# Decays of the first block from halves of 64 tokens: one running product of 512 columns per sequence, outer products and a masked spread on TensorE

## Chip, cores, metric

One core of one Trainium2 chip. The metric is the device time of one execution in microseconds, taken over several executions. All runs quoted here are of the state that the records call fast. Where two kernels are compared, the ratio is the mean time of one kernel's fast runs over that of the other's fast runs of the same rounds, so it is not quite the ratio of the medians beside it. "Faster" and "slower" mean below that the 95% interval of the ratio leaves out 1. The last three runs of the table of experiments ran on another chip, where the kernel before took 406.69 us; the eight before them on one chip.

## The reference

Two parts, one after the other. A Mamba-2 scan turns `x`, `a`, `B`, `C` (4 sequences, 8 heads, 768 tokens) into `y`, and a gated feed-forward block turns `y` into the output.

```python
# scan, per sequence and head: state decays by a[t], clipped to 1e-6..1
# y[i] = sum over j <= i of (C[i].B[j]) * (a[j+1]*...*a[i]) * x[j]   (plus the carried state)
h = x @ w_in            # 3072 x 256  @  256 x 2048
g = h * np.cos(h)
return (g @ w_out)      # 3072 x 2048 @ 2048 x 256
```

## The kernel before

Tokens go in six blocks of 128. The feed-forward block of block c runs while the scan of block c+1 is made, so only the scan of block 0 stands alone, ahead of everything else: this is the head that the change rewrites. For each sequence it needs the matrix `lam`, for 8 heads the 128 x 128 decays between every two tokens, got as running products along the columns. The decays `a` have to stand in all 128 partitions for that; TensorE spreads them with a column of ones. `fill` is a matmul without use, there to keep the array busy.

```python
def fill(dst, times=1):
    for _ in range(times):
        PE.matmul(dst, lhsT=ones, rhs=ones..., start=True, stop=True, ...)

def spread_a(b, tags):            # 4 heads to a bank of PSUM, two banks to a sequence
    ...
    for h in range(HH):
        r = (b_ * H + t * HH + h) * NC
        PE.matmul(a_ps[:, h], lhsT=ident[0:RB, r:r + 1].to_broadcast([RB, P]),   # RB = 96 rows
                  rhs=cut[:, u], start=(h == 0), stop=True, ...)

def decays(c, b, t):              # one scan of 512 columns: 4 heads x 128 tokens
    V.tensor_tensor_scan(out=lam[c, b][:, hs]..., data0=rows_..., data1=unit...,
                         initial=0.0, op0=ALU.mult, op1=ALU.add)
    ...

# turn: transposes B and C of a sequence (tp), ScalarE copies them (cT, bcT)
# intra: g = B.C on TensorE, then m = g * lam on VectorE (two instructions of 512 columns)
# finish: y = x.m on TensorE, copied to yT by ScalarE
# first: hp = w_in.yT, the first matmul of the feed-forward block
# grade, join: the weights, held as 64-bit floats, are made fp32 piece by piece

fill(bank([P, 4, P], "warm", "o"), 2)
spread_a(0, (None, "h"))
decays(0, 0, 0)
decays(0, 0, 1)
spread_a(1, ("o", "o"))
turn(0, 0)
decays(0, 1, 0)
decays(0, 1, 1)
intra(0, 0)
...                               # cut: the same for sequences 2 and 3
finish(0, 3, "o", 2)
...
for n in range(NC * NF + LAG):    # the body: first(n), gate(n), second(n - LAG), scan of block c+1
    ...
```

## Time and profile before

| | before |
|---|---|
| time, median of 6 runs | 407.28 us (407.03 to 407.63) |
| profiled span | 404.6 us |
| first hp matmul starts | 22.55 us |
| from there to the end | 382.1 us |

The prediction shows the main lines. Two more rows of the table by stretches matter later (columns: stretch, its length, busy us and count for PE, weight loads, VectorE, ScalarE, GpSimd, then granted clock, DMA share, GB/s):

```profile
6.00:12.00 6.00, 5.13 (x47) 4.52 (x46) 5.59 (x7) 0.78 (x3) 0.82 (x2) 1.00 1.00 108
12.00:18.00 6.00, 5.70 (x73) 4.04 (x72) 5.35 (x7) 3.36 (x10) 1.44 (x3) 1.00 1.05 340
```

### The profile page before, as it was taken

How to read it: one execution, taken by the hardware profiler on the slowest of the kernel's cores; microseconds unless marked ns; L12 is line 12 of the kernel's file. 1: busy time of each engine (PE TensorE's matmuls, PEld its weight loads, DVE VectorE, ACT ScalarE, POOL GpSimd, SP SyncE). 2: the span in 40 equal slices, each digit the busy share in tenths (PEclk: the TensorE clock that was granted, in tenths of full speed). 3: DMA queues.
4: the chain of work that ended last, by engine and by line, in shares of the span. 5: the costliest groups of instructions: out<-in, count | busy, mean ns of one | idle time of the engine just before them, and what ended most of it. 6: DMA issues, size and time to landing. Idle time of an engine off the chain costs nothing.

```text
span 404.6 us, 5703 instructions
## 1 busy us (share of the span) xinstructions
PE 397.9 (98%) x2166; PEld 254.3 (63%) x2166; DVE 257.7 (64%) x396; ACT 173.7 (43%) x329; POOL 48.1 (12%) x78
## 2 busy tenths in 40 slices
PE   8999999999999999999999999999999999999996
PEld 5646665666666666666656666666656565666664
DVE  6989999936666645676654666664566764433342
ACT  2576656534343434434334433433434343433332
POOL 2266655400000000000000000000000000000000
PEclk9999999999999999999999999999999999999999
DMA  7989999691111094110168211120100000100001
GB/s 112 301 229 221 221 272 146 169 104 53 52 54 52 17 143 75 53 52 2 52 107 77 75 31 53 52 78 3 52 2 0 0 2 0 53 0 0 2 0 53
DMA packets 106651, 30.55 MB, mean 75 GB/s; under 512 B 75328, under 2 KB 102528, under 8 KB 106624
## 3 DMA queue, kind: packets, MB, share of 16 engines
q1 hardware_dynamic: 106096, 29.92, 35.7%
q8 instruction: 17, 0.28, 0.3%
q10 hardware_dynamic: 528, 0.26, 0.2%
q14 instruction: 10, 0.08, 0.1%
HBM read 26.84 MB, written 3.34 MB: 75 GB/s over the span
## 4 chain that ended last, share of the span: by engine, by line
PE 97%; ACT 1%; DVE 1%; issue 0%; DVEq 0%
PE hp L378 42%; PE o L406 41%; PE g L309 4%; PE y L334 3%; PE y L325 2%; PE a_ps L258 2%; PE warm L94 1%; PE tp L291 1%; PE tp L290 1%; PE s_ps L351 0%; PE y L94 0%; ACT cT L295 0%; ACT w L389 0%; DVE m L313 0%; DVE gT L391 0%
## 5 line engine op out<-in xcount | busy, mean ns | idle before, releaser
L378 PE MATMUL hp<-yT,w_in 128*128 128x512 f32 x384 | 184.6, 604 | 0.7 <-DVE gT L391 0.7
L406 PEld LDWEIGHTS o<-w_out,gT 128*128 128x128 f32 x768 | 145.9, 190 | 59.9 <-issue 44.0
L406 PE MATMUL o<-w_out,gT 128*128 128x256 f32 x768 | 181.1, 379 | 0.0
L382 ACT ACTIVATE k<-hp 128x512 int32<-128x512 f32 x96 | 57.4, 598 | 125.9 <-PE hp L378 125.8
L384 DVE SCALAR_TENSOR_TENSOR w<-hp,k 128x512 f32<-128x512 f32 x96 | 66.0, 687 | 69.7 <-ACT k L382 68.4
L391 DVE TENSOR_TENSOR gT<-hp,w 128x512 f32<-128x512 f32 x96 | 66.3, 690 | 65.4 <-ACT w L389 65.4
L378 PEld LDWEIGHTS hp<-yT,w_in 128*128 128x128 f32 x384 | 67.9, 190 | 58.1 <-issue 53.8
L389 ACT ACTIVATE w<-w,quarter 128x512 f32<-128x512 f32 x96 | 69.3, 722 | 76.6 <-DVE w L384 76.6
L274 DVE TENSOR_TENSOR_SCAN lam<-arow,unit 128x512 f32<-128x512 f32 x40 | 49.0, 1226 | 0.0
L313 DVE TENSOR_TENSOR m<-g,lam 128x512 f32<-128x512 f32 x48 | 30.7, 681 | 0.9 <-PE g L309 0.7
L283 POOL TENSOR_TENSOR sc<-bc,lam 128x128 f32<-128x128 f32 x20 | 8.3, 413 | 122.5 <-DVE lam L274 79.5
L295 ACT ACTIVATE cT<-tp,slot 128x128 f32<-128x128 f32 x48 | 14.7, 356 | 9.4 <-PE tp L291 9.4
L309 PE MATMUL g<-cT,bcT 32*128 32x256 f32 x192 | 17.3, 426 | 1.2 <-ACT bcT L297 1.2
L334 PE MATMUL y<-m,xr 128*32 128x128 f32 x384 | 15.8, 279 | 0.2 <-DVE m L313 0.2
L369 POOL TENSOR_TENSOR state<-whole,slot 128x64 f32<-128x64 f32 x16 | 5.5, 343 | 79.3 <-DVE whole L366 79.3
L195 DVE SCALAR_TENSOR_TENSOR mag<-words,mag 128x512 uint32<-128x512 uint32 x16 | 13.2, 823 | 0.6
L175 POOL TENSOR_SCALAR mag<-mag 128x512 f32<-128x512 f32 x16 | 12.5, 783 | 7.5 <-ACT mag L174 7.5
L339 ACT COPY yT<-y 128x256 f32<-128x256 f32 x24 | 8.9, 371 | 10.2 <-PE y L334 10.1
L309 PEld LDWEIGHTS g<-cT,bcT 32*128 32x128 f32 x192 | 7.7, 182 | 8.8 <-issue 5.8
L334 PEld LDWEIGHTS y<-m,xr 128*32 128x32 f32 x384 | 8.8, 109 | 5.4 <-issue 3.6
L174 ACT ACTIVATE mag<-words 128x512 f32<-128x512 f32 x16 | 10.9, 683 | 1.7 <-DMA words<-in_moe_w_in_dram 1.7
L199 POOL TENSOR_TENSOR w_out<-mag,last 128x512 uint32<-128x512 uint32 x8 | 10.2, 1275 | 8.8 <-DVE mag L195 6.8
(49 smaller groups left out, 146.0 us busy)
## 6 DMA issues: line engine op xcount, KB each, us to landing
arow<-a_cut SPq DMA_DIRECT2D x20, 512.0 KB
words<-in_moe_w_in_dram SPq DMA_DIRECT2D x8, 512.0 KB
words<-in_moe_w_out_dram SPq DMA_DIRECT2D x8, 512.0 KB
out_dram<-ob SPq DMA_DIRECT2D x10, 256.0 KB
xr<-in_x_dram SPq DMA_DIRECT2D x4, 512.0 KB
along<-a_all SPq DMA_DIRECT2D x20, 64.0 KB
xr<-in_x_dram SPq DMA_DIRECT2D x8, 128.0 KB
bc<-in_B_dram SPq DMA_DIRECT2D x4, 256.0 KB
```

The source lines that it names most:

```text
L195: V.scalar_tensor_tensor(out=bits, in0=high, scalar=0xC0000000, in1=bits, op0=ALU.bitwise_and, op1=ALU.bitwise_or)
L274: V.tensor_tensor_scan(out=lam[c, b][:, hs].rearrange("p h i -> p (h i)"), data0=rows_.rearrange("p h i -> p (h i)"), data1=unit.rearrange ...
L295: ACT.activation(cT[:, t], tp[:, 1], AF.Copy, scale=slot[:, t:t + 1])
L309: PE.matmul(g[u // 2][:, u % 2, 0:2 * P], lhsT=bcT[r, 0], rhs=cT[r].rearrange("p t i -> p (t i)"), start=True, stop=True)
L313: V.tensor_tensor(out=m[:, hs].rearrange("p (k t) i -> p k (t i)", k=2), in0=g[u][:, :, 0:2 * P], in1=l[:, hs].rearrange("p (k t) i -> p k ...
L334: PE.matmul(y[32 * q:32 * q + 32, t], lhsT=xr[:, b, h], rhs=m[:, h], start=(c == 0 and t == 0), stop=True, tile_position=(0, 32 * q), skip ...
L378: PE.matmul(hp[n], lhsT=w_in[:, k, f * P:(f + 1) * P], rhs=yT[c][:, k], start=(k == 0), stop=(k == KT - 1))
L382: ACT.activation(k, hp[n], AF.Copy, bias=0.25, scale=INV_2PI)
L384: V.scalar_tensor_tensor(out=w, in0=hp[n], scalar=INV_2PI, in1=k, op0=ALU.mult, op1=ALU.subtract)
L389: ACT.activation(cos, cos, AF.Sin, bias=quarter, scale=TWO_PI)
L391: V.tensor_tensor(out=gT[n], in0=hp.pop(n), in1=cos, op=ALU.mult)
L406: PE.matmul(o[c][b], lhsT=g[:, b * P:(b + 1) * P], rhs=w_out[:, f], start=(f == 0 and (last or b % 2 == 0)), stop=(f == NF - 1), skip_grou ...
```

## The change

A block of 128 tokens is cut into two halves of 64. The two diagonal quarters of `lam` (both tokens in the same half) are made by one scan of 512 columns: the first half in partitions 0 to 63, the second in 64 to 127, 8 heads side by side. The quarter between the halves is an outer product: (decay from j to the end of the first half) times (decay from the start of the second half to i); TensorE makes it for 8 heads in one matmul, from operands in which masks leave each head only its own row. So VectorE needs four long scans instead of eight. The spread, too, is now a matmul over 32 masked rows (4 sequences x 8 heads). The core of the diff:

```diff
-    # cut: spread_a as it was, 56 passes of lhsT 96x128, rhs 96x128
+    def spread_a(b):
+        spread[b] = ps = bank([P, H, W], "a_ps", "h")
+        for t in range(2):
+            PE.matmul(ps[t * W:(t + 1) * W], lhsT=those[:, b], rhs=a0s[:, t], start=True,
+                      stop=True, tile_position=(0, t * W), skip_group_check=True)
+    def decays0(b):
+        lam[0, b] = l = scan.tile([P, 2, H, W], FP32, tag="lam", bufs=3, name="lam")
+        V.tensor_tensor_scan(out=l[:, 0]..., data0=spread.pop(b)..., data1=unit0..., ...)
+        G.tensor_copy(out=l[W:P, 1], in_=l[W:P, 0])
+        G.memset(l[W:P, 0], 0.0)
+    def cross(b):
+        ps = bank([W, H, W], "l_ps", "o")
+        PE.matmul(ps, lhsT=fros[:, b], rhs=tos, start=True, stop=True)
+        ACT.copy(out=lam[0, b][0:W, 1], in_=ps)
+        weigh(0, b)
 ...
+    # masks mine, those; short scans to, fro; masked operands a0s, fros, tos, all of 32 partitions
-    fill(bank([P, 4, P], "warm", "o"), 2)
+    fill(bank([P, 4, P], "warm", "o"), 3)
+    spread_a(1)
     turn(0, 0)
+    spread_a(2)
+    decays0(0)
+    decays0(1)
+    cross(0)
+    intra(0, 0, mult=False)
+    decays0(2)
+    cross(1)
+    spread_a(3)
+    gated(0, 0)
+    decays0(3)
+    turn(0, 1, "h")
+    cross(2)
+    finish(0, 0, "o", 1)
+    intra(0, 1)
 ...
+    cross(3)
+    turn(0, 2, "h")
     grade(*order[0])
 ...
+    join(*order[0])
     grade(*order[2])
-    join(*order[0])
```

The clip of the whole `a` and its stores move behind this, and the weights' first piece is fetched ahead of sequence 3's inputs.

More of the change, by code (lines that the diff above doesn't have):

```diff
@@ L63 @@
     LAG = 2
-    HP = H // 2
+    W = P // 2
+    NR = NB * H
     const = ctx.enter_context(tc.tile_pool(name="const", bufs=1))
@@ L132, in load_along @@
                 .to_broadcast([H, N, P]))
-    row0 = const.tile([P, HH, P], FP32, name="row0")
-    nc.scalar.dma_start(out=row0, in_=a[0, 0:HH, 0:P].unsqueeze(0).to_broadcast([P, HH, P]))
+    row0 = const.tile([P, H, W], FP32, name="row0")
+    a0 = const.tile([NR, P], FP32, name="a0")
+    nc.scalar.dma_start(out=a0, in_=a[:, :, 0:P].rearrange("b h p -> (b h) p"))
+    for t in range(2):
+        nc.sync.dma_start(out=row0[t * W:(t + 1) * W],
+                          in_=a[0, :, t * W:(t + 1) * W].unsqueeze(0).to_broadcast([W, H, W]))
     a_in = const.tile([RB, NU, P], FP32, name="a_in")
-    nc.sync.dma_start(
-        out=a_in, in_=a.rearrange("(u b) h (c p) -> (b h c) u p", u=NU, p=P))
     w_in = const.tile([P, KT, DF], FP32, name="w_in")
@@ L204 @@
         load(0, (b, b + 1))
-    for n in (0, 2, 1, 3, 4, 5):
+        if b == 1:
+            nc.sync.dma_start(
+                out=a_in, in_=a.rearrange("(u b) h (c p) -> (b h c) u p", u=NU, p=P))
+        if b == 2:
+            fetch(*order[0])
+    for n in (2, 1, 3, 4, 5):
         fetch(*order[n])
@@ L215 @@
     V.tensor_copy(out=unit, in_=ident.unsqueeze(1).to_broadcast([P, HH, P]))
+    unit0 = const.tile([P, H, W], FP32, name="unit0")
+    for t in range(2):
+        ts = slice(t * W, (t + 1) * W)
+        V.tensor_copy(out=unit0[ts], in_=ident[ts, ts].unsqueeze(1).to_broadcast([W, H, W]))
+    mine = const.tile([NR, H], FP32, name="mine")
+    G.tensor_tensor(out=mine, in0=ident[0:NR, 0:H], in1=ident[0:NR, H:2 * H], op=ALU.add)
+    for b in range(2, NB):
+        G.tensor_tensor(out=mine, in0=mine, in1=ident[0:NR, b * H:(b + 1) * H], op=ALU.add)
+    those = const.tile([NR, NB, W], FP32, name="those")
+    G.memset(those, 1.0)
+    G.affine_select(out=those, in_=those, pattern=[[-H, NB], [0, W]], compare_op=ALU.is_ge,
+                    fill=0.0, base=0, channel_multiplier=1)
+    G.affine_select(out=those, in_=those, pattern=[[H, NB], [0, W]], compare_op=ALU.is_ge,
+                    fill=0.0, base=H - 1, channel_multiplier=-1)
     own = const.tile([P, H], FP32, name="own")
-    V.memset(own, 1.0)
+    G.memset(own, 1.0)
     G.affine_select(out=own, in_=own, pattern=[[-N, H]], compare_op=ALU.is_ge,
@@ L224 @@
     slot4 = const.tile([P, HH], FP32, name="slot4")
-    V.tensor_tensor(out=slot4, in0=own[:, 0:HH], in1=own[:, HH:H], op=ALU.add)
+    G.tensor_tensor(out=slot4, in0=own[:, 0:HH], in1=own[:, HH:H], op=ALU.add)
     slot = const.tile([P, 2], FP32, name="slot")
-    V.tensor_tensor(out=slot, in0=slot4[:, 0:2], in1=slot4[:, 2:4], op=ALU.add)
-    cut = const.tile([RB, NU, P], FP32, name="cut")
-    G.tensor_scalar(out=cut, in0=a_in, scalar1=1.0, scalar2=1e-6, op0=ALU.min, op1=ALU.max)
-    G.memset(cut[:, :, 0:1], 0.0)
@@ L233 @@
-    la = const.tile([RB, NU, P], FP32, name="la")
-    V.tensor_scalar(out=la, in0=a_in, scalar1=1.0, scalar2=1e-6, op0=ALU.min, op1=ALU.max)
-    for dst, src in ((a_cut, cut), (a_all, la)):
-        nc.sync.dma_start(out=dst.rearrange("(u b) h (c p) -> (b h c) u p", u=NU, p=P), in_=src)
-    V.tensor_scalar(out=row0, in0=row0, scalar1=1.0, scalar2=1e-6, op0=ALU.min, op1=ALU.max)
+    G.tensor_tensor(out=slot, in0=slot4[:, 0:2], in1=slot4[:, 2:4], op=ALU.add)
+    ACT.activation(const.tile([P, 1], FP32, name="sine"), quarter, AF.Sin)
@@ new lines @@
+    clip = dict(scalar1=1.0, scalar2=1e-6, op0=ALU.min, op1=ALU.max)
+    V.tensor_scalar(out=a0, in0=a0, **clip)
+    to = const.tile([NR, W], FP32, name="to")
+    V.tensor_tensor_scan(out=to, data0=a0[:, W:P], data1=ones[0:NR, 0:W], initial=1.0,
+                         op0=ALU.mult, op1=ALU.mult)
+    fro = const.tile([NR, W], FP32, name="fro")
+    V.memset(fro, 1.0)
+    V.tensor_tensor_scan(out=fro[:, W - 2::-1], data0=a0[:, W - 1:0:-1],
+                         data1=ones[0:NR, 0:W - 1], initial=1.0, op0=ALU.mult, op1=ALU.mult)
@@ new lines @@
+    a0s = const.tile([NR, 2, H, W], FP32, name="a0s")
+    V.tensor_tensor(
+        out=a0s,
+        in0=a0.rearrange("p (t i) -> p t i", t=2).unsqueeze(2).to_broadcast([NR, 2, H, W]),
+        in1=mine.unsqueeze(1).unsqueeze(3).to_broadcast([NR, 2, H, W]), op=ALU.mult)
+    V.memset(a0s[:, :, :, 0:1], 0.0)
+    fros = const.tile([NR, NB, W], FP32, name="fros")
+    V.tensor_tensor(out=fros, in0=fro.unsqueeze(1).to_broadcast([NR, NB, W]), in1=those,
+                    op=ALU.mult)
+    tos = const.tile([NR, H, W], FP32, name="tos")
@@ L238 @@
+    for h in range(H):
+        ACT.activation(tos[:, h], to, AF.Copy, scale=mine[:, h:h + 1])
+    V.tensor_scalar(out=row0, in0=row0, **clip)
     V.memset(row0[:, :, 0:1], 0.0)
-    ACT.activation(const.tile([P, 1], FP32, name="sine"), quarter, AF.Sin)
     scaled, lam, reach, state, part, yT = {}, {}, {}, {}, {}, {}
@@ L246, in heads, with weigh @@
         return slice(b * H, (b + 1) * H)
-    spread = {}
-    def spread_a(b, tags):
-        u, b_ = b // (NB // NU), b % (NB // NU)
-        spread[b] = [] if b else [row0]
-        for t in range(len(spread[b]), 2):
-            a_ps = bank([P, HH, P], "a_ps", tags[t])
-            for h in range(HH):
-                r = (b_ * H + t * HH + h) * NC
-                PE.matmul(a_ps[:, h], lhsT=ident[0:RB, r:r + 1].to_broadcast([RB, P]),
-                          rhs=cut[:, u], start=(h == 0), stop=True, skip_group_check=True)
-            spread[b].append(a_ps)
+    spread = {0: row0}
+    def spread_a(b):
+        spread[b] = ps = bank([P, H, W], "a_ps", "h")
+        for t in range(2):
+            PE.matmul(ps[t * W:(t + 1) * W], lhsT=those[:, b], rhs=a0s[:, t], start=True,
+                      stop=True, tile_position=(0, t * W), skip_group_check=True)
+    def decays0(b):
+        lam[0, b] = l = scan.tile([P, 2, H, W], FP32, tag="lam", bufs=3, name="lam")
+        flat = "p h i -> p (h i)"
+        V.tensor_tensor_scan(out=l[:, 0].rearrange(flat), data0=spread.pop(b).rearrange(flat),
+                             data1=unit0.rearrange(flat), initial=0.0,
+                             op0=ALU.mult, op1=ALU.add)
+        G.tensor_copy(out=l[W:P, 1], in_=l[W:P, 0])
[5 more added lines that the diff above has]
+        weigh(0, b)
+    def weigh(c, b):
+        scaled[c, b] = sc = scan.tile([P, H, N], FP32, tag="sc", bufs=NB, name="sc")
+        l = lam[c, b][:, :, P - 1:P] if c > 0 else lam[c, b][:, 1, :, W - 1:W]
+        G.tensor_tensor(out=sc, in0=raw[c][0][:, 0, heads(b)],
+                        in1=l.to_broadcast([P, H, N]), op=ALU.mult)
     def reaches(c, b):
@@ L272, in decays @@
         hs = slice(t * HH, (t + 1) * HH)
-        rows_ = spread[b][t] if c == 0 else arow[c, b][:, hs]
+        rows_ = arow[c, b][:, hs]
         V.tensor_tensor_scan(
@@ L280, in decays @@
             return
-        scaled[c, b] = sc = scan.tile([P, H, N], FP32, tag="sc", bufs=NB, name="sc")
-        G.tensor_tensor(out=sc, in0=raw[c][0][:, 0, heads(b)],
-                        in1=lam[c, b][:, :, P - 1:P].to_broadcast([P, H, N]), op=ALU.mult)
+        weigh(c, b)
     def turn(c, b, tag=None):
@@ L300, in turn, with intra @@
         part[c, b] = (bcT, cT)
-    def intra(c, b):
+    def intra(c, b, mult=True):
         bcT, cT = part[c, b]
-        m = scan.tile([P, H, P], FP32, tag="m", name="m")
-        l = lam.pop((c, b))
         g = [pair("g") for _ in range(2)]
@@ L308, in intra, with gated, of @@
             r = slice(32 * u, 32 * u + 32)
-            PE.matmul(g[u // 2][:, u % 2, 0:2 * P], lhsT=bcT[r, 0],
-                      rhs=cT[r].rearrange("p t i -> p (t i)"), start=True, stop=True)
+            rhs = (cT[r].rearrange("p t i -> p (t i)") if c > 0 else
+                   cT[r].rearrange("p t (s i) -> p s t i", s=2))
+            PE.matmul(g[u // 2][:, u % 2, 0:2 * P], lhsT=bcT[r, 0], rhs=rhs,
+                      start=True, stop=True)
+        part[c, b] = (bcT, g)
+        if mult:
+            gated(c, b)
+    def gated(c, b):
+        bcT, g = part[c, b]
+        l = lam.pop((c, b))
+        m = scan.tile([P, H, P] if c > 0 else [P, 2, H, W], FP32, tag="m", name="m")
+        def of(t, u):
+            hs = slice(u * HH, (u + 1) * HH)
+            return (t[:, hs].rearrange("p (k t) i -> p k (t i)", k=2) if c > 0 else
+                    t[:, :, hs].rearrange("p s (k t) i -> p k s (t i)", k=2))
         for u in range(2):
-            hs = slice(u * HH, (u + 1) * HH)
-            V.tensor_tensor(out=m[:, hs].rearrange("p (k t) i -> p k (t i)", k=2),
-                            in0=g[u][:, :, 0:2 * P],
-                            in1=l[:, hs].rearrange("p (k t) i -> p k (t i)", k=2), op=ALU.mult)
+            in0 = g[u][:, :, 0:2 * P]
+            if c == 0:
+                in0 = in0.rearrange("p k (s i) -> p k s i", s=2)
+            V.tensor_tensor(out=of(m, u), in0=in0, in1=of(l, u), op=ALU.mult)
         part[c, b] = (bcT, m)
@@ L333, in finish @@
             q, t = h % 4, h // 4
-            PE.matmul(y[32 * q:32 * q + 32, t], lhsT=xr[:, b, h], rhs=m[:, h],
+            PE.matmul(y[32 * q:32 * q + 32, t], lhsT=xr[:, b, h], rhs=m[:, h] if c > 0 else m[:, :, h],
                       start=(c == 0 and t == 0), stop=True, tile_position=(0, 32 * q),
@@ L418, in second @@
             nc.sync.dma_start(out=rows_[:, 2 * i:2 * i + 2, c, :], in_=ob)
-    fill(bank([P, 4, P], "warm", "o"), 2)
-    spread_a(0, (None, "h"))
-    decays(0, 0, 0)
-    decays(0, 0, 1)
-    spread_a(1, ("o", "o"))
-    turn(0, 0)
-    decays(0, 1, 0)
-    decays(0, 1, 1)
-    intra(0, 0)
-    spread_a(2, ("h", "h"))
-    decays(0, 2, 0)
-    decays(0, 2, 1)
-    turn(0, 1)
-    finish(0, 0, "o")
-    intra(0, 1)
+    fill(bank([P, 4, P], "warm", "o"), 3)
+    spread_a(1)
+    turn(0, 0)
+    spread_a(2)
[5 more added lines that the diff above has]
+    cross(1)
+    cut = const.tile([RB, NU, P], FP32, name="cut")
+    la = const.tile([RB, NU, P], FP32, name="la")
+    spread_a(3)
[4 more added lines that the diff above has]
+    finish(0, 0, "o", 1)
+    intra(0, 1)
+    V.tensor_scalar(out=la, in0=a_in, **clip)
+    G.tensor_scalar(out=cut, in0=a_in, **clip)
+    G.memset(cut[:, :, 0:1], 0.0)
+    for dst, src in ((a_cut, cut), (a_all, la)):
+        nc.sync.dma_start(out=dst.rearrange("(u b) h (c p) -> (b h c) u p", u=NU, p=P), in_=src)
+    cross(3)
+    turn(0, 2, "h")
     grade(*order[0])
-    spread_a(3, ("o", "h"))
-    decays(0, 3, 0)
-    decays(0, 3, 1)
-    turn(0, 2, "h")
     finish(0, 1, "o", 1)
```

## The prediction

> **What bounds the kernel now.** I read the activity rows of the page first, then the table of busy time by stretches, then the chain that ended last, in order of time, for the first 32 us, then the timeline of each engine there, and the groups with shapes kept apart for durations.
>
> ```profile
> PE   8999999999999999999999999999999999999996
> DVE  6989999936666645676654666664566764433342
> ```
>
> TensorE (PE) is busy in nearly every slice of 10 us. Busy is not bound, so the stretches come next (columns: stretch, length, then busy us and count for PE, weight loads, VectorE, ScalarE, GpSimd, then clock, DMA share, GB/s):
>
> ```profile
> 18.00:24.00 6.00, 5.83 (x53) 2.79 (x53) 5.80 (x10) 3.75 (x9) 3.74 (x4) 1.00 0.90 257
> 24.00:30.00 6.00, 5.31 (x46) 2.67 (x45) 4.76 (x9) 5.07 (x9) 3.49 (x5) 1.00 0.81 242
> 30.00:36.00 6.00, 6.00 (x24) 3.94 (x23) 5.97 (x12) 3.25 (x6) 4.60 (x4) 1.00 0.98 195
> 60.00:80.00 20.00, 20.00 (x111) 12.45 (x110) 19.10 (x32) 11.99 (x24) 9.78 (x12) 1.00 0.93 154
> ```
>
> From 30 us on PE has no idle time. Three rounds of the second stage repeat every 12.7 us there (hp starts at 39.1 and 51.8), and their PE work is 3 x (1.91 + 1.73) plus about 1.8 of block work, 12.7. So the body is PE's own work and this change does not touch it. What can move is the start of the body, the first hp matmul at 22.55. That head is a chain through four sequences:
>
> ```profile
> 4.91 3.29 PE a_ps L258 x24
> ...
> 10.00 1.98 PE a_ps L258 x16
> ...
> 13.78 1.98 PE a_ps L258 x16
> ...
> 17.00 0.72 PE g L309 x8
> ...
> 18.35 0.69 DVE m L313
> 19.05 0.04 issue
> 19.09 0.43 PE y L334 x8
> 19.52 0.64 PE g L309 x8
> 20.16 1.06 PE y L94 x4
> 21.22 0.74 PE y L334 x16
> 21.96 0.63 PE warm L94 x2
> 22.59 1.92 PE hp L378 x4
> ```
>
> Here the reader is to see that the head, too, is mostly PE in its program order: spreads of the decays (a_ps), transposes, g, y. VectorE enters at 17.75 to 19.05 (m of sequence 2) and, hidden behind the filler matmuls at 20.16, at 20.19 to 21.48 (m of sequence 3). It is nearly full as well, with 5.80 of 6 us. Thus two engines are close to the bound in the head, and relief on one pays only until the other holds.
>
> [...]
>
> ```profile
> L265 DVE TENSOR_TENSOR_SCAN reach<-along,ones 128x128 f32<-128x128 f32 x20 | 10.3, 516 | 0.0
> L274 DVE TENSOR_TENSOR_SCAN lam<-a_ps,unit 128x512 f32<-128x512 f32 x7 | 8.1, 1206 | 0.3 <-PE a_ps L258 0.3
> ```
>
> 384 more columns cost 690 ns, 1.8 ns per column. [...] the trace has 681 (m) and 690 (gT). [...] sixteen y passes of 128 columns in four groups take 0.64 us with their latency, although one such pass takes 0.124 us in a_ps (1.98/16). [...] four filler passes of 512 columns from 1.12 on take 3.78 us, the same width later 1.91; the clock row, full throughout, does not show it.
>
> **Removed.** Of eight scans of 512 columns for block 0, four go: 4 x 1.2 = 4.8 us of VectorE. The 56 spread passes go from PE: 3.29 + 1.98 + 1.98 = 7.25 us. The masks (slot and own) move from VectorE to GpSimd, 0.4 us.
>
> **Added on VectorE before the first scan.** Two copies for unit0, 0.43 each as the present copy (L215); the clip of a0, about 0.2; two scans of 64 columns, about 0.3 to 0.4 each by the slope above; [...] small memsets, 0.2. Row a0 should land near 2.9, as a_in does now (wait ends at 3.09). [...] the clip of row0 (0.43, L237) and its memset 6.1. So the first scan starts at about 6.1 against 4.94 now: 1.2 of the 4.8 us are given back at once, and VectorE nets about 3.5 us less.
>
> **Added on PE.** Three spreads, each two fp32 matmuls of 512 columns. One fp32 matmul is two passes of 0.43 (hp: 1.91/4, start to start 0.43), so 0.87; the two column tiles go side by side, about 1.0 with weight loads. Four outer products (cross), 0.87 to 0.9 each. Sum 3 x 1.0 + 4 x 0.9 = 6.6 us against 7.25: **PE gains almost nothing.** One more filler of 512 columns stands at the start and one of 256 columns (two passes, 0.46 with their loads) before y of sequence 0.
>
> **Added elsewhere.** ScalarE: four copies of 64x512 from PSUM (about 0.5 each, from ob's 0.565) and eight small ones (0.25 each, before 6 us, harmless). GpSimd: per sequence one copy of 64x512 (0.6 to 0.9 from L175) and one memset (0.5), behind the scans, with room. DMA: row0 keeps its 256 KB but in pieces of half the size; the weights' first piece goes ahead of sequence 3's inputs. DMA is full from 2 to 22 us before and after; the last weights and the stores of a_cut keep their time, and the decays of block 1, first read at 33.5, have some microseconds to spare.
>
> **The new path in time**, all starts estimated from the durations above. The six passes of the filler: four start 0.85 apart from 1.12, the next at 4.7 and 5.55, ending near 6.2 as the clock comes up. Then in PE's program order: spread 1 to 7.2, transpose 0 (0.22) 7.4, spread 2 8.4, cross 0 9.3, g0 (0.64 to the next start now) 9.9, cross 1 10.8, spread 3 11.8, transpose 1 12.0, cross 2 12.9, filler 13.4, y0 (0.4) 13.8, g1 14.4, cross 3 15.3, transpose 2. Nothing waits long there: scans 0 to 2 run at 6.1 to 10.0, m0 till 11.3, scan 3 from 11.9 to 13.1, and VectorE then **idles** for g1 until about 14.5. ScalarE copies cross 3 (till 15.9), then cT and bcT of sequence 2 (0.8 from start to end, 8.45 to 9.23 now): g2 starts at 16.75, now 17.00. From there the old structure holds: m2 is over 1.8 later, y2 and the release of g's banks give g3 at 2.35 to 2.45 after g2 (17.00 to 19.45 now), 19.1; the first joining of weights stands before m3 as now (1.2 us); hp follows g3 by 3.1 (19.45 to 22.55): **22.2**. With spreads and crosses at 0.87 each it is 21.7. So the PE reading saves 0.35 to 0.85 us, not 3.5.
>
> **Rivals.** (a) VectorE is what bounds the head; then its net relief of 3.5 us arrives whole and hp starts near 19.0, total 403.9. For it: the two gaps in the chain at VectorE and its 5.8 of 6 us. Against it: the 9 us of PE work counted above lie in order between 6.2 and 15.3. I give it 0.15, a halfway outcome (PE gets ahead of its estimate, -1.5 to -2.5) 0.2. (b) ScalarE's order becomes the bound: cross copies stand before cT and bcT, and 2 x 1.2 us of weight conversion (pitch 0.59 each activation) lie between sequence 2's and the end; hp near 22.5, no change. For it: the conversion of the first piece, which was done at 15 us, now follows transpose 2. 0.25. (c) The side-by-side tiles do not hold[...]: three times 0.86 more, hp near 24, total 409. Against it: y's passes. 0.08. (d) The earlier body runs into transfers not yet landed: the saving is hidden; with only 0.5 us to lose it makes 407.4 at worst.
>
> **Range and chances.** The body moves one for one with hp. 0.5 x (-0.6) + 0.15 x (-3.5) + 0.2 x (-1.5 to -2) + the rest near 0 or +1 gives about -1.0: 407.4 - 0.9 = **406.5 us**, 8 in 10 between 404.7 and 407.9. 2% is 8.1 us, more than a third of the head, so within 2% has 0.97, faster 0.02, slower 0.01.
>
> **What would show it.** Right: four scans from about 6 us at 1.2 each; the spread in four passes within 1.1 us; a0s 1.2 us; PE without long gaps from 6 to 15 us; VectorE idle ahead of m1 and m2, waiting for g; first hp between 21.5 and 22.3; the body's length from the first hp to the end, 382.1 now, the same within 0.3. Wrong: hp before 20.5 (rival a), or cT of sequence 2 waiting behind other ScalarE work (b), spreads of 1.8 us (c), or a DMA wait at 25 to 35 us and a longer body (d).

The sum for the first scan came to 5.2 us for the end of a0s, 5.6 for that of fros and, with the clip and the memset, 6.1. The trace before gives about the same two costs as an estimate: operations of two inputs on VectorE take 0.292 us at 128 columns (bcT) and 0.681 at 512 (m; gT 0.690), which is 1.01 ns per column, so 1.20 us for the 1024 columns of a0s and 0.42 for the 256 of fros.

## The result and the profile after

The changed kernel takes 413.49 us (median of 6 runs, 411.61 to 414.74), the kernel before 407.28. The ratio is 1.0148, 95% interval 1.0112 to 1.0183. It is slower by 6 us, and its runs spread over 3 us, those of before over 0.6. They fall in two groups: 411.6 to 412.3, with a mean granted clock of 0.983 to 0.988, and 414.7 with 0.978 to 0.979. The profiled one is of the second group.

The activity rows of its page:

```profile
PE   8999999999999999999999999999999999999996
DVE  7258999964766763767673576764566665444442
PEclk9569999999999999999999999999999999999999
```

TensorE's row is as full as before. The row below is what is new: in the second and third slices the granted clock is at 5 to 6 tenths. By stretches, same columns as above:

```profile
6.00:12.00 6.00, 6.00 (x25) 1.78 (x25) 4.71 (x6) 1.36 (x4) 4.48 (x9) 0.87 0.98 138
12.00:18.00 6.00, 6.00 (x10) 1.30 (x7) 1.54 (x2) 1.94 (x5) 2.32 (x5) 0.50 0.97 226
18.00:24.00 6.00, 6.00 (x39) 2.62 (x42) 1.49 (x3) 2.11 (x6) 1.03 (x4) 0.50 0.99 351
24.00:30.00 6.00, 6.00 (x64) 3.17 (x53) 3.56 (x6) 4.45 (x11) 2.14 (x3) 0.71 0.68 142
```

TensorE counts as busy all the time, and its clock is halved from 10.5 to 27.5 us. VectorE, the engine that was to be relieved, works 1.5 of 6 us and waits for TensorE. The trace's clock record has these moments: full from 7.06, half from 10.47, full again from 27.54 us. The stretch at half clock is 17.07 us. The chain that ended last shows each piece at both speeds (columns: start us, us, what):

```profile
8.22 1.00 PE a_ps L297 x4
9.23 0.85 PE l_ps L314 x2
...
12.74 1.71 PE a_ps L297 x3
...
15.06 1.89 PE l_ps L314 x2
...
20.29 1.90 PE l_ps L314 x2
...
23.66 1.01 PE y L407 x16
24.67 1.24 PE g L369 x8
```

An outer product (l_ps) takes 0.85 us at 9.23 and 1.9 at 15.06 and 20.29; y takes 1.01, in the kernel before 0.57 to 0.74. The first hp, in the timeline:

```profile
31.10 1.10 PE L451 MATMUL hp<-yT,w_in 128*128 128x512 f32 x2
```

It starts at 31.10, before at 22.55, 8.55 later. The body from there to the end takes 413.0 - 31.10 = 381.9 us, before 382.1. So the whole loss of this execution lies in the head.

### The profile page after: what moved, and what is told of

Its sections match the earlier page's. It is cut to its first block, busy times and chain, and to the rows that moved or that the text cites. A ratio compares the mean times of both kernels' runs of the same rounds, so it can differ in the third digit from the quotient of the medians.

```text
span 413.0 us, 5679 instructions
## 1 busy us (share of the span) xinstructions
PE 407.8 (99%) x2134; PEld 252.0 (61%) x2134; DVE 256.2 (62%) x398; ACT 177.9 (43%) x341; POOL 56.8 (14%) x95
## 4 chain that ended last, share of the span: by engine, by line
PE 96%; DVE 2%; POOL 0%; issue 0%; ACT 0%; DVEq 0%; POOLq 0%
PE hp L451 41%; PE o L479 40%; PE g L369 4%; PE y L407 3%; PE y L398 2%; PE l_ps L314 2%; PE warm L95 1%; PE a_ps L297 1%; PE tp L350 1%; PE tp L351 1%; DVE mag L199 1%; PE y L95 0%; PE s_ps L424 0%; DVE mag L197 0%; POOL w_in L203 0%
## 5 line engine op out<-in xcount | busy, mean ns | idle before, releaser
L369 PE MATMUL g<-cT,bcT 32*128 32x256 f32 x192 | 18.5, 452 | 0.0
L407 PE MATMUL y<-m,xr 128*32 128x128 f32 x384 | 16.7, 293 | 0.0
L203 POOL TENSOR_TENSOR w_in<-mag,last 128x512 uint32<-128x512 uint32 x8 | 10.3, 1287 | 11.5 <-DVE mag L199 11.5
```

Of the source, the lines that this page charges most:

```text
L203: G.tensor_tensor(out=dst.bitcast(U32), in0=bits.rearrange("p (k f) -> p k f", k=k), in1=last.rearrange("p (k f) -> p k f", k=k), op=ALU.add)
L369: PE.matmul(g[u // 2][:, u % 2, 0:2 * P], lhsT=bcT[r, 0], rhs=rhs, start=True, stop=True)
L407: PE.matmul(y[32 * q:32 * q + 32, t], lhsT=xr[:, b, h], rhs=m[:, h] if c > 0 else m[:, :, h], start=(c == 0 and t == 0), stop=True, tile_p ...
```

## The experiments

The stretches of the clock record are 3.41, 17.07 and 385.7 us long in this trace, 1, 5 and 113 times 3.413 us, and 399.4 us in the kernel before, 117 times; such a step is called a window below. **Theory A**: the clock is halved because the new matmuls use few rows and columns of the array. TensorE is busy, but with 32 rows of 128 and, in the outer products, 64 columns of 128. **Theory B**: the array waits between instructions and so counts as idle, or what counts is the data, which are mostly zeros under the masks. Against the first half of B speaks already that the kernel before waited more (5.13 of 6 us busy) and kept its clock.

For theory A I estimated the use of the array in the changed kernel's one window at full clock, 7.06 to 10.47, from the durations of its chain: spreads 1.4 us (0.86 for the second by the passes' pitch of 0.43, the rest of the first) on a quarter of the array (32 rows, and 128 columns by two tiles side by side), transposes 0.22 us in full, an outer product 0.86 us on an eighth, g 0.3 us in full (four tiles of 32 rows): (0.35 + 0.22 + 0.11 + 0.3)/3.41 = 0.29, rounded to 0.3. In the same way I had 0.56 for the kernel before; a recount below gives 0.50 for its emptiest window.

All times, in the order in which they ran (first hp and span from the profiled execution):

| kernel | median us | ratio to before, interval | first hp | span less first hp |
|---|---|---|---|---|
| before (first 6 runs) | 407.28 | | 22.55 | 382.1 |
| changed | 413.49 | 1.0148 (1.0112 to 1.0183) | 31.10 | 381.9 |
| rows128 | 407.22 | 1.0001 (0.9986 to 1.0016) | 23.45 | 382.1 |
| before_rows32 | 413.89 | 1.0169 (1.0134 to 1.0204) | 31.41 | 382.6 |
| fillers | 410.73 | 1.0092 (1.0073 to 1.0112) | 26.99 | 382.1 |
| spread128 | 407.99 | 1.0017 (1.0002 to 1.0031) | 24.02 | 382.1 |
| cross128 | 407.68 | 1.0012 (0.9997 to 1.0028) | 24.12 | 382.1 |
| nofill | 406.56 | 0.9984 (0.9969 to 0.9998) | 23.06 | 382.1 |
| reordered | 405.75 | 0.9965 (0.9953 to 0.9978) | 21.82 | 381.8 |
| reordered2 | 405.57 | 0.9971 (0.9953 to 0.9989) | 23.55 | 381.8 |
| rows64 | 406.96 | 1.0010 (0.9993 to 1.0027) | 22.76 | 382.1 |
| cols128 | 412.11 | 1.0129 (1.0114 to 1.0144) | 28.26 | 381.8 |
| after_again | 414.72 | 1.0177 (1.0141 to 1.0213) | 30.83 | 382.2 |

The last column is the point of the table: in thirteen profiles the body takes 381.8 to 382.6 us. Whatever a kernel gains or loses, it does so ahead of the first hp.

### rows128: zeros in 96 more rows

```diff
-    a0 = const.tile([NR, P], FP32, name="a0")
+    a0 = const.tile([P, P], FP32, name="a0")
+    V.memset(a0[NR:2 * NR], 1.0)
+    V.memset(a0[2 * NR:P], 1.0)
     # mine, those, to, fro, a0s, fros, tos likewise [P, ...]; the masks make the added rows zero
```

> The changed kernel with the operands of its spreads and outer products padded from 32 to 128 partitions by rows of zeros; same passes, same result. Theory A, the array's clock is halved because what runs from 7 to 10.5 us uses few rows and columns of the array: the granted clock is 1.00 from about 7 us to the end, the first hp starts near 22.2 instead of 31.1, total 406.3 to 407.5. Theory B, the clock falls because TensorE waits between instructions, or because most of the data are zeros: nothing changes, 411.6 to 414.7.

The result is correct. The granted clock is 1.00 from 6.02 us to the end, and the 6 us are gone: 407.22 against 407.23 in the same rounds. The added rows hold zeros only, so neither the passes nor the useful data changed, and theory B falls in both its halves. From its chain:

```profile
7.76 1.01 PE a_ps L299 x4
8.77 0.85 PE l_ps L316 x2
...
12.50 1.00 PE l_ps L316 x2
...
15.35 1.00 PE l_ps L316 x2
```

The outer products stay at 0.85 to 1.00 us. The first hp starts at 23.45, where 22.2 was expected. And this is the fair test of the change's own idea: **with the clock kept, it gains nothing.** Its timeline shows why:

```profile
15.45 1.29 DVE L390 TENSOR_TENSOR m<-g,lam 128x512 f32<-128x512 f32 x2 [1.99 <-PE g L371]
...
18.58 1.29 DVE L390 TENSOR_TENSOR m<-g,lam 128x512 f32<-128x512 f32 x2 [1.64 <-PE g L371]
...
23.45 3.67 PE L453 MATMUL hp<-yT,w_in 128*128 128x512 f32 x8
...
28.77 1.52 PE L453 MATMUL hp<-yT,w_in 128*128 128x512 f32 x3 [1.07 <-DVE gT L466]
```

VectorE, with four scans less, idles 1.99 and 1.64 us for g (the bracket gives the idle time ahead of an instruction and what ended it). TensorE's program order holds the head.

### before_rows32: the same loss in the kernel before

```diff
-                PE.matmul(a_ps[:, h], lhsT=ident[0:RB, r:r + 1].to_broadcast([RB, P]),
-                          rhs=cut[:, u], start=(h == 0), stop=True, skip_group_check=True)
+                r = r % 32
+                PE.matmul(a_ps[:, h], lhsT=ident[0:32, r:r + 1].to_broadcast([32, P]),
+                          rhs=cut[0:32, u], start=(h == 0), stop=True, skip_group_check=True)
```

> The kernel before with its spread contracting over 32 rows instead of 96 (wrong decays on purpose, same passes and columns). Theory A: the clock falls to 0.50 about 9.5 us after the start for some windows, the first hp comes 4 to 9 us later, total 411 to 416. Theory B: 407.3 as the kernel before.

The result is wrong: heads get other heads' decays. The time is 413.89 us, as theory A expects, with nothing of the change in the kernel but the 32 rows. From its chain:

```profile
4.91 5.42 PE a_ps L259 x24
...
13.05 3.39 PE a_ps L259 x16
```

The kernel before has 3.29 and 1.98 there. One thing differs from what I wrote: in the profiled execution the clock did not rise and fall, it did not rise at all before 27.84 us. Its clock record begins with this rise, and the profile shows 1.00 for the 27 us ahead of it and a mean clock of 0.999. The durations show the half clock; the clock figure does not. It is the same in the kernel before, whose record begins at 6.05 us: the stretch from 0 to 6 us shows 1.00, and four passes of the filler took 3.78 us there, four of hp, as wide, 1.92 later. Two of the four runs (414.93 and 415.68 us) have this mean clock of 0.999; the other two (412.63 and 412.86) have 0.979, as of a clock that rose and fell. None of these two was profiled.

### fillers: more work, more speed

```diff
+    def busy(ps):
+        fill(ps.rearrange("p (k h) i -> p k (h i)", k=4)[:, 0:2], 1)
         spread[b] = ps = bank([P, H, W], "a_ps", "h")
+        busy(ps)
 ...                                  # and the same ahead of each outer product
```

> The changed kernel with one filler matmul of 128 rows, 128 columns and 256 moving columns ahead of each of the three spreads and four outer products: 7 x 0.43 = 3.0 us more work on TensorE. Theory A: the clock stays at 1.00, and hp starts near 24 to 25, total 408.5 to 410. If the fall has a cause outside the array's activity, the fillers only add: 414 to 418.

The clock is full from 4.94 us on, and the kernel is 2.8 us **faster** than the changed one although TensorE does seven matmuls more. At 410.73 us it is 0.7 above what I expected. The fillers took 0.43 us three times and 0.63 four times in its chain, 3.8 us and not 3.0; 26.99 - 3.8 = 23.2 is close to where rows128 has its hp, 23.45.

### spread128, cross128, rows64, cols128: how much is enough

```diff
# spread128: rows128, but cross with lhsT=fros[0:NR, b], rhs=tos[0:NR]
# cross128:  rows128, but spread_a with lhsT=those[0:NR, b], rhs=a0s[0:NR, t]
# rows64:    rows128, but [0:W] (64 rows) in both
# cols128:   the changed kernel, 32 rows, but
-    fros = const.tile([NR, NB, W], FP32, name="fros")
+    fros = const.tile([NR, NB, 2, W], FP32, name="fros")
+    G.memset(fros[:, :, 1], 0.0)      # 64 more columns of weights, zeros
```

> As rows128, but only the spreads are padded, the outer products stay at 32 rows and 64 columns. By the share of the array used in a window of 3.41 us, weighted by rows and columns, I estimate 0.6 in the window from 7 us on (0.3 in the changed kernel, 0.56 in the kernel before): theory A expects the clock to hold and 406.3 to 407.5; a loss of clock here would put the limit above 0.6 or show that the outer products count for more than their area.

> As rows128, but only the four outer products are padded to 128 rows; the spreads stay at 32. By area the window from 7 us on is used about 0.38 (changed kernel 0.3, spread128 0.6). If what counts is area and the limit for keeping the clock lies between 0.3 and 0.6, this decides on which side of 0.38: clock held and 406.5 to 408, or lost and 410 to 415.

> As rows128, but padded to 64 rows only, spreads and outer products alike. By area the window from 7 us on is used about 0.42, a little more than in cross128 (0.38), which kept its clock. If area is what counts: clock held, 407 to 408.2. If whole rows of the array have to be fed in some part of the window: clock lost, 410 to 415.

> The changed kernel with its outer products at 32 rows as they are, but 128 columns instead of 64, the second half of the weights being zeros. By area the window is used about 0.32 (changed kernel 0.30, cross128 0.38 by rows). I expect the clock to be lost in at least some runs, 410 to 415, whether rows or area count; a clock held in all would say that columns count for much more than area.

By my estimate of the area used in the window from 7 us on: 0.30 (changed) and 0.32 (cols128) lose the clock, 0.38 (cross128), 0.42 (rows64) and 0.6 (spread128) keep it. cols128 took 412.11 us in a narrow band (411.37 to 412.42), with a stretch of 13.65 us at half clock. But these figures are for one window at one place, and each run's windows lie elsewhere: cols128 kept its clock up for two windows, from 4.65 on, and lost it after the one from 8.07 to 11.48.

So the count was made again for every window of the thirteen profiles, with the windows placed by each run's own clock record. A pass of 512 columns counts for its pitch (0.43 us at full clock, twice that at half), up to 0.16 us before its recorded end (it is recorded with 0.59 us), with the share of the array that it uses. These are estimates:

| the clock after the window | share of the array used |
|---|---|
| was full, fell (3 windows) | 0.27 (after_again), 0.30 (changed), 0.33 (cols128) |
| was full, stayed | the lowest: 0.34 (cross128), 0.39 (nofill), 0.40 (fillers), 0.42 (rows64) |
| was half, rose (16 windows) | the lowest: 0.77 (rows64), 0.80 (reordered2) |
| was half, stayed (22 windows) | the highest: 0.76 (before_rows32), 0.71 (reordered2), 0.71 (changed) |

By this estimate area puts all windows of the thirteen profiles in order: a full clock was kept above about a third of the array, a half clock left only above about three quarters. Rows alone do not: by the same count a window with 0.44 of the rows in use lost the clock in the changed kernel, and one with 0.40 kept it in nofill. The second limit would explain the five windows at half clock in the changed kernel: their shares are 0.23, 0.26, 0.71, 0.56 and 0.80, and the clock rose after the last. Both limits are fitted to profiles already seen and no run was made to test them; the margins (0.33 to 0.34, 0.76 to 0.77) are narrower than the count is exact, though the order stays with 0.10 or 0.20 us in place of 0.16.

spread128 and cross128 are 0.5 to 0.8 us slower than rows128 with the clock held in their profiles; theirs came up at 6.69 and 6.90 us, that of rows128 at 6.02 and that of rows64 (hp at 22.76) at 3.96, which fits the order, but I did not test whether it is the whole cause. In eleven of the thirteen profiles the full clock came at 3.96 to 7.06 us, in reordered2 at 10.52 and in before_rows32 at 27.84, there with TensorE 5.13 of 6 us busy from 6 to 12 us and 6.00 of 6 after that.

### after_again: the two groups of times

> The changed kernel as it is, on this chip. [...] 411.6 to 414.7 again, in steps of about 1.5 to 3 us, and the profile should show a stretch at 0.50 whose length is a whole number of windows of 3.41 us.

Three runs at 414.7 to 414.8 and one at 411.65; the profiled one has a stretch of 17.07 us at half clock, from 9.50 us on. 3.41 us of full clock come before it, as in the first profile. 17.07 is five times 3.413, and the 13.65 of cols128 four times. The faster group's mean clock of 0.983 means about (1 - 0.983) x 2 x 410 = 14 us at half clock, four such windows; the 0.986 and 0.988 of two of the first runs mean 10 to 11.5 us, about three. The groups thus seem to differ by a window or two. This is not shown: I have no profile of a run of the faster group.

### nofill, reordered, reordered2: a version that beats both

```diff
# nofill: rows128, and
-    finish(0, 0, "o", 1)
+    finish(0, 0, "o")                 # also for sequences 1 and 2
# reordered: nofill, and g ahead of the y before it, both transposes ahead of the last
# outer product, the second piece graded before the first is joined
+    intra(0, 1)
+    finish(0, 0, "o")
 ...
+    turn(0, 2, "h")
+    turn(0, 3, "h")
+    cross(3)
+    grade(*order[0])
+    intra(0, 2)
+    finish(0, 1, "o")
+    grade(*order[2])
+    join(*order[0])
+    intra(0, 3)
+    finish(0, 2, "o")
# reordered2: reordered, and
-    fill(bank([P, 4, P], "warm", "o"), 3)
+    fill(bank([P, 4, P], "warm", "o"), 2)
```

> rows128 without the three filler matmuls ahead of y of sequences 0, 1 and 2. If with a full clock the head is bound by TensorE's program order, 0.63 + 0.43 us go from the chain (the third lies in a wait): first hp at 22.4 instead of 23.45, total 406.2. If VectorE, ScalarE or the weights' conversion bound it: 407.2 as rows128. If the fillers were needed for the clock: a loss of clock and over 409.

> nofill, with g of a sequence ahead of y of the one before, both remaining transposes ahead of the last outer product, and the second weight piece graded before the first is joined, as in the kernel before. If TensorE's order and the latency behind it bound the head: hp near 21.9, total 405.6. If the conversion of the weights (VectorE's joins at 20 to 26 us) bounds the second pair of hp matmuls, the gap before it grows by what hp gains and the total stays at 406.2 or above.

> reordered with two instead of three filler matmuls at the start. The spread could start at 5.5 instead of 6.3 and all behind it 0.8 us earlier: 404.9. But the array may then come to full clock a window later, as the first windows hold less work: then 406 to 409 and the runs spread by more than 1 us.

nofill gains 0.7 us on rows128 by its ratio (0.9984 against 1.0001), two thirds of the 1.06 expected; but the two intervals overlap, so the gain over rows128 is likely and not shown. Its hp came at 23.06, and its clock was full from 6.60 on: with the operands of the spreads and outer products padded, it was kept without these fillers. With them gone, the next thing shows: TensorE waits 0.44 us ahead of g of sequence 2 for bcT from ScalarE. reordered has its hp at 21.82 (expected 21.9) and takes 405.75 us (expected 405.6), the ratio to before is 0.9965 (0.9953 to 0.9978). It is faster than both kernels, by 0.35% than the one before, with five runs in a band of 0.6 us (the profiled one, of 405.33, is the fastest). Its timeline of TensorE ahead of the second pair of hp matmuls:

```profile
21.82 3.67 PE L453 MATMUL hp<-yT,w_in 128*128 128x512 f32 x8
25.43 0.65 PE L426 MATMUL s_ps<-xr,sc 128*32 128x64 f32 x32
26.77 1.96 PE L453 MATMUL hp<-yT,w_in 128*128 128x512 f32 x4 [0.69 <-DVE gT L466]
```

The wait for gT is 0.69 us as in the kernel before, in rows128 1.07. I put this 0.4 us down to a second, small loss in the change: with the first weight piece joined before the second is graded, GpSimd adds the first piece (1.29 us in rows128) before it clips the second, and VectorE waits 0.59 us for that. It was not tested by itself. reordered2, whose interval lies below 1 as well, starts with a filler less: four of its six runs lie at 405.1 to 405.7 and two at 406.9 and 407.1; in the profiled one, of 407.12, the clock came up only at 10.52 us. Its ratio, 0.9971 (0.9953 to 0.9989), cannot be told from that of reordered; what the third filler is seen to buy is the narrower band.

## Why the prediction was wrong

**The step that failed** is "The new path in time": it gives every piece on TensorE the duration at full clock, from "ending near 6.2 as the clock comes up" on, as if a clock once up stayed up. The runs show that it came up at 7.06 us, fell 3.4 us later and stayed halved for five windows, 17.07 us. The prediction has the slow filler passes at the start (3.78 us for four, 1.91 later at the same width) and puts them into the filler's six, and never asks whether the new, smaller matmuls keep the array in use. None of the four rivals has it; (c), 409 us, came nearest in time, and its mechanism did not occur: the spread's four passes took 1.00 us at full clock, side by side. Cause and size are shown by rows128 (nothing but rows of zeros, ratio 1.0148 to 1.0001; all ten runs of the changed kernel took over 411.6 us, all four of rows128 under 407.6) and by before_rows32 (1.0169 with the 32 rows alone, although in its profile the clock failed to rise instead of falling).

**What held.** That the head and not the body moves one for one with the first hp: last column of the table. That PE gains almost nothing and VectorE's relief of 3.5 us does not arrive: rows128, with VectorE idle 1.99 and 1.64 us ahead of m1 and m2. Of the single costs, the scans took 1.22 to 1.24 us, a0s 1.19 (1.2 expected), and the first scan began at 6.08 (6.1 expected). The 0.97 for a time within 2% of the kernel before held too (1.0148). Rival (a) is refuted. (b) did not bind in rows128, where ScalarE idles 1.29 us for the last outer product ahead of sequence 2's transposes; but once the fillers are gone it does: in nofill the chain goes through the copy of that outer product, then cT and bcT, and TensorE waits 0.44 us. Of (d) nothing is seen, the body kept its length.

**What was mis-sized even at full clock.** hp was put at 22.2 or 21.7 and came at 23.45 in rows128. The filler before y0 was put at 0.46 and took 0.63, outer products 1.00 (0.9), y 0.57 (0.4), two transposes 0.37 (0.22): durations read off as start to start in streams of one kind, where each change of kind cost 0.1 to 0.2 us more here. Over the thirteen pieces ahead of sequence 2's transposes that made 1 us (16.35 in rows128 against 15.3, 0.2 of it from the later start), and the total came out at 407.2, where 406.5 was predicted. Two sums in "Rivals" and "Range and chances" do not close, without weight for the result: the chances 0.5, 0.15, 0.2, 0.25 and 0.08 make 1.18, and a sum of about -1.0 is used as -0.9.

## What to carry to other kernels

Making matmuls smaller did not only shorten them here: after 3.4 us in which TensorE was busy with a small part of its array (0.30 by my estimate, the spreads and outer products with 32 of 128 rows) it had half its clock for 17 us, and the busy row looked as full as ever (6.00 of 6 us). So look at the granted clock and at the same instruction's duration early and late before believing any sum of durations, and if short contractions must stand alone, pad them with rows of zeros, which kept the clock here (rows128, 407.22 us instead of 413.49) and cost TensorE no time (an outer product at full clock took 0.85 to 1.00 us with them, 0.85 in the changed kernel and 1.00 in spread128 without). And before relieving one of two nearly full engines, add up the other one's work in program order; here that sum said from the start that there was little to gain.
